# Linear attention plus feed-forward: a tail load on another queue, weights loaded twice, one transpose by DMA and a regrouped fold

## The chip, the cores and the metric

The kernel runs on one core of a Trainium2 chip. A core has a matrix engine (TensorE, PE in the profile; its weight loads are PEld), VectorE (DVE), ScalarE (ACT), GpSimd (POOL) and SyncE (SP), which run their own instruction streams and meet through semaphores, and 16 DMA engines, which move data on orders that SP and ACT issue. Each engine takes its instructions strictly in order. The metric is the device time of one execution in microseconds (us), as a median over runs.

## The reference

A normalised input goes into two branches whose outputs are added to the input. S = 2048 rows, D = 448 columns, 16 heads of 28, FF = 1792, all bf16:

```python
xn = layernorm(x)                                   # per row
q, k, v = split(xn @ wqkv)                          # 16 heads of 28 columns each
pq, pk = q @ w_phi[h], k @ w_phi[h]                 # the feature map, per head
phi_q = concat(softmax(pq), softmax(-pq)); phi_k = the same of pk
kv, z = phi_k^T v, sum of phi_k over the rows
o = (phi_q @ kv) / (phi_q . z + 1e-6)
out = x + o @ wo + silu(xn @ w1) @ w2
```

## The kernel before

The rows are worked on in 8 pairs of 128-row tiles (256 rows each). TensorE runs through these stages:

1. Normalisation of a pair (`ln_pair`): statistics and scaling on VectorE and GpSimd into `xn_sb` (two buffers), then a transpose into `xnT`, whose layout is two row groups of 64 partitions by seven blocks (448 = 7 x 64). Pairs 0 to 3 are transposed by TensorE (seven instructions, line 508) into PSUM bank 6 and evicted by VectorE (line 668). Pairs 4 to 7 are transposed by a DMA on SP's queue (line 561).
2. First feed-forward product (`ffn1_chunk`): xn @ w1, whose 14 column tiles go to silu on ScalarE. Column tiles 0 to 7 are done pair by pair (128-wide matmuls), 8 to 13 for two pairs at once (256-wide). Pairs 0 to 3 come in the first 36 us, pairs 4 to 7 later.
3. The fold (`fold`): the feature map is multiplied into the query and key weights. `wT` holds the transposed weights (eight DMA transposes from HBM, line 597; indices 4 to 7 for the keys and 0 to 3 for the queries), `BDphi` the block-diagonal feature map. Each of the two has four output blocks, done in groups of two with PSUM banks 4 and 7 (eight matmuls a group), evicted by ScalarE.
4. The K and V stage (`k_macro`, `q_group`, `k_acc`), which begins at 35.65 us in the trace and is called the value stage below: per pair the products for K, exponentials, V with its eviction on VectorE (line 800), the sums over the features, and the accumulation of kv. It takes until some 78 us.
5. The query stage with the second feed-forward product and the output, to the end.

Since TensorE contracts over 128 partitions in two halves of 64, a weight with 448 rows is stored twice, halves exchanged: a main load brings rows 0 to 383 into blocks 0 to 2 (`load_main`), a copy exchanges the 64-partition halves into blocks 3 to 5 (`swap`, two copies, one per half, each on ScalarE or VectorE), and the last 64 rows are loaded twice into block 6 (`load_tail`). This holds for w1 (`w1_sb`), the value weights (columns VO of `W_sb`) and wo; for the folded weights the swap follows the fold.

All loads of the first stages are issued by SP in the order in which they are written, but for the tail of w1's columns 0 to 512, which ACT issues behind its table load. The tail of the other columns of w1 is one pair of loads of 160 KB, issued directly behind the main load of columns 512 to 1024.

The order of every engine's instructions comes from a planner (`schedule`) that simulates the program with assumed durations: at each step it takes, among the operations that could start about first, the one with the lowest priority number and then the lowest number in the program, and fills gaps with others. A load's landing is planned from an assumed rate. TensorE also has 26 filler multiplications of a zero tile (`zz`, lines 545 to 551): 12 of 512 columns at the start and 14 of 256 columns that the planner puts into gaps. In the trace nine of the 14 stand behind pair 0's transposes, three and two on either side of pair 1's.

Of the kernel before, what the change touches and what calls it, by code (L numbers as in the profile page):

```python
# [8 lines left out]
ACTF = mybir.ActivationFunctionType  # L9
# [135 lines left out]
class _Prog:  # L145
# [72 lines left out]
    def schedule(self):  # L218
# [30 lines left out]
        for e, t0, per in (("sp", -100.0, 550.0), ("act", 1500.0, 600.0)):  # L249
            for q in loads[e]:  # L250
                t0 += ops[q[0]].dur if ops[q[0]].name == "wT_dt" else per
                q[2] = t0
        now, stalled = 0.0, False
# [111 lines left out]
def bass_parallel_sum__linear_kernel_hedgehog__dense_activation_silu__prompt_kernel(  # L365
# [20 lines left out]
    with es:  # L386
# [14 lines left out]
        WC = VO + D  # L401
# [70 lines left out]
        def d_dve(n, mode=1):  # L472
            return n * 1.042 / mode + 150.0
# [72 lines left out]
        for c0, c1 in ((0, 32), (32, 512)):  # L546
            P.op("dve", 450 + (c1 - c0) * 0.3, lambda e, c0=c0, c1=c1: e.memset(zz[:, c0:c1], 0.0), writes=[zz[:, c0:c1]], name="zz")
        for n, rows, cols, dur in ((12, 128, 512, 430.0), (0, 128, 512, 215.0), (14, 128, 256, 109.0)):
            for i in range(n):
                mm(banks[5][0:rows, 0:cols], zz[:, 0:rows], zz[:, 0:cols], True, True, "warm")  # L550
                P.ops[-1].dur = dur
# [8 lines left out]
        def transpose_dma(dst, src, name):  # L560
            P.dma(lambda e: e.dma_start_transpose(out=dst, in_=src), 128 * 896 * 2, reads=[src], writes=[dst], name=name, dur=1230.0)
# [4 lines left out]
        def load_main(dst, src, c0, c1, d0, name):  # L566
            load(dst[:, 0:3, d0:d0 + c1 - c0], src[0:384, c0:c1].rearrange("(k p) f -> p k f", p=128), 384 * (c1 - c0) * 2, name)

        def load_tail(dst, src, c0, c1, d0, name, eng="sp"):
            for h in range(2):  # L570
                o = load(dst[64 * h:64 * h + 64, d0:d0 + c1 - c0], src[384:448, c0:c1], 64 * (c1 - c0) * 2, name, eng, half=True)
                if eng == "act":
                    o.odeps.add(table_op.id)

# [13 lines left out]
        load_main(w1_sb, B_w1, 512, 1024, 512, "w1_1")  # L588
        load_tail(w1_sb[:, 6], B_w1, 512, FF, 512, "w1_1t")
        load_main(w1_sb, B_w1, 1024, 1408, 1024, "w1_2a")  # L590
        load_main(w1_sb, B_w1, 1408, FF, 1408, "w1_2b")
        load_x(2, 3)
# [12 lines left out]
        load_x(6, 8)  # L605
        load_main(W_sb, A_wqkv, 2 * D, 3 * D, VO, "wv")
        load_tail(W_sb[:, 6], A_wqkv, 2 * D, 3 * D, VO, "wvt")

# [8 lines left out]

        BK_F = [4, 7]
        first_ve, first_xn, first_ev, second_tr, second_ev, last_mm = [], [], [], [], [], []
# [38 lines left out]
        def ln_tr(p, bk):  # L658
            sl = p % NXN
            dstx = xnT[:, :, p, :]  # L660
            if p >= 4:
                transpose_dma(dstx, xn_sb[:, sl, :], "xnT_dt")
                return
            tp = bank16[bk][:, 0:896].rearrange("p (j c) -> p j c", j=KB)
            transpose_many([(tp[:, j, :], xn_sb[:, sl, 128 * j:128 * j + 128]) for j in range(KB)], "xnT_tr")
            if p == 1:
                second_tr.append(P.ops[-1])
            o = P.op("dve", d_dve(896, 2), lambda e: e.tensor_copy(dstx, tp), reads=[tp], writes=[dstx], name="xnT_ev")  # L668
            if p < 2:
                (first_ev, second_ev)[p].append(o)  # L670
# [56 lines left out]
        def fold():  # L727
# [9 lines left out]
            for a0 in range(0):  # L737
# [3 lines left out]
                for i in range(2):  # L741
                    act(wT[0:KP, a0 + 2 * i:a0 + 2 * i + 2], tps[i], ACTF.Identity, "wT_ev")
            swap(W_sb, VO, WC, ("dve", "dve"))
            for qk in (1, 0):
                for k0 in range(0, 4, 2):
                    parts = []
                    for i in range(2):
                        parts += [(banks[BK_F[i]][:, g * KP:(g + 1) * KP], wT[0:KP, qk * 4 + g, (k0 + i) * 128:(k0 + i + 1) * 128],
                                   BDphi[:, g, :], True, True) for g in range(G)]
                    mm_many(parts, "fold_mm")  # L750
                    for i in range(2):
                        dst, src = W_sb[:, k0 + i if k0 + i < 3 else 6, KO:VO], banks[BK_F[i]][:, 0:D]
                        if qk == 0:
                            dst = W_sb[:, k0 + i if k0 + i < 3 else 6, 0:QW].rearrange("p (g r f) -> p g r f", g=G, r=2)[:, :, :, 0:56]
                            src = src.rearrange("p (r g f) -> p g r f", r=2, g=G)
                        act(dst, src, ACTF.Identity, "fold_ev")
                swap(W_sb, KO if qk else 0, VO if qk else QW, ("dve", "dve"))

        ln_pair(0)
        swap(w1_sb, 0, 256, ("act", "act"))  # L760
        swap(w1_sb, 256, 512, ("act", "act"))
        ffn1_chunk(0, 1, 0, 4)
# [3 lines left out]
        ffn1_chunk(0, 1, 4, 8)  # L766
        last_mm[-1].odeps |= {q.id for q in second_tr}
        n0 = len(P.ops)
# [14 lines left out]
        ln_pair(5)  # L783
        ln_pair(6)
        ln_pair(7)

        def k_unit(p, j, b0, name):
# [334 lines left out]
```

## Time and profile before

| | us |
|---|---|
| median of 3 runs (157.63 to 158.75) | 158.08 |
| the profiled execution | 157.24 |
| its span | 155.5 |
| TensorE busy in the span | 150.7 (97%) |
| VectorE, ScalarE, GpSimd busy | 102.6, 74.2, 63.7 |
| chain that ended last: share of TensorE | 89% |
| start of the value stage (first matmul of `xnT` against folded weights) | 35.65 |

The span is the time from the first to the last instruction in the trace; 1.7 us of the execution lie around it. All times in the trace count from the start of the span. "idle before" in brackets is the time that an engine stood still ahead of an instruction, and behind it what ended that, as far as the trace shows. The chain is followed back from the last instruction: at each step to what released it, or to the instruction before on its engine.

### The profile page before, as it was taken

To read this page: it belongs to the slowest core of one execution; us is meant where nothing else is said; L and a number is where in the kernel's file an instruction comes from. 1 tells how busy PE (TensorE), PEld (TensorE's weight loads), DVE (VectorE), ACT (ScalarE), POOL (GpSimd) and SP (SyncE) were. 2 spreads that over 40 slices of the span, in tenths; PEclk is the share of its full clock that TensorE was granted. 3 is DMA by queue.
4 is the path that set the end of the run, shared out by engine and by line. 5 is a ranking of instruction groups with operands and counts; after the bars stand their busy time and mean duration, and the time that the engine had idled before them with its cause. 6 is when DMAs were issued, how large, how long until landed. Compare 5 with 4: busy or idle time off the path is not lost.

```text
span 155.5 us, 6049 instructions
## 1 busy us (share of the span) xinstructions
PE 150.7 (97%) x2751; PEld 98.3 (63%) x2751; DVE 102.6 (66%) x198; ACT 74.2 (48%) x82; POOL 63.7 (41%) x73
## 2 busy tenths in 40 slices
PE   6889999999999999999999999999999999999994
PEld 2378899795444546446878898655555555556553
DVE  5897977995978875889098769667985930022042
ACT  3778757878789688785955566800000000000000
POOL 5320306379388775479601453366146060000000
PEclk9999999999999999999999999999999999999999
DMA  5999678303724223300000083300840143041011
GB/s 152 268 277 115 110 180 249 62 17 69 99 53 139 49 93 95 93 0 6 4 4 4 0 63 63 59 4 0 124 118 4 28 115 98 0 118 63 0 59 59
DMA packets 23353, 12.11 MB, mean 78 GB/s; under 512 B 16160, under 2 KB 23200, under 8 KB 23328
## 3 DMA queue, kind: packets, MB, share of 16 engines
q1 hardware_dynamic: 23168, 11.60, 34.9%
q8 instruction: 21, 0.34, 0.9%
q10 hardware_dynamic: 160, 0.13, 0.3%
q14 instruction: 4, 0.03, 0.1%
HBM read 6.22 MB, written 1.84 MB: 52 GB/s over the span
## 4 chain that ended last, share of the span: by engine, by line
PE 89%; DVE 7%; POOL 2%; issue 1%; POOLq 0%
PE psum L490 84%; PE psum L483 4%; PE psum L508 1%; DVE st L621 1%; POOL rstd L637 1%; DVE KVZ L862 1%; DVE kvs L854 1%; DVE kvs L855 1%; DVE mask L532 1%; DVE xn_sb L650 1%; DVE mv L629 0%; DVE xnT L668 0%; DVE ve L635 0%; DVE KVZ L537 0%; POOL ident L519 0%
## 5 line engine op out<-in xcount | busy, mean ns | idle before, releaser
L490 PE MATMUL psum<-xnT,w_sb 64*128 64x256 bf16 (+1 forms) x1008 | 45.6, 246 | 0.5 <-DVE xn_sb L650 0.5
L490 PEld LDWEIGHTS psum<-xnT,w_sb 64*128 64x128 bf16 x1008 | 39.2, 94 | 5.0 <-ACT w_sb L515 0.6
L515 ACT ACTIVATE ar<-psum 128x896 bf16<-128x896 f32 (+2 forms) x38 | 32.0, 880 | 10.9 <-PE psum L490 10.8
L916 POOL TENSOR_TENSOR scr<-scr 128x384 bf16<-128x384 f32 (+3 forms) x32 | 20.1, 660 | 31.8 <-DVE scr L911 26.0
L808 POOL TENSOR_TENSOR ar<-ar,Rk 128x1792 bf16<-128x1792 bf16 (+1 forms) x9 | 25.8, 2877 | 10.1 <-DVE Rk L807 9.1
L960 DVE TENSOR_TENSOR out_sb<-psum,x_sb 128x448 bf16<-128x448 f32 (+2 forms) x17 | 9.5, 593 | 23.6 <-PE psum L490 20.5
L490 PE MATMUL psum<-ar,xnT 64*128 64x448 bf16 x224 | 22.7, 349 | 0.0
L490 PE MATMUL psum<-w_sb,hT_lo 64*128 64x448 bf16 x224 | 22.3, 349 | 0.0
L515 ACT ACTIVATE eq<-psum 128x1024 bf16<-128x1024 f32 x16 | 15.5, 1025 | 6.1 <-PE psum L490 6.0
L805 DVE TENSOR_REDUCE Sk<-ar 128x64 f32<-128x1792 bf16 (+1 forms) x9 | 16.2, 1804 | 2.5 <-ACT ar L515 2.5
L490 PEld LDWEIGHTS psum<-ar,xnT 64*128 64x128 bf16 x224 | 10.7, 94 | 10.4 <-DVE ar L800 0.4
L911 DVE TENSOR_TENSOR scr<-psum,Gq 128x896 f32<-128x896 f32 x16 | 16.9, 1087 | 0.4
L515 ACT ACTIVATE hT_lo<-psum 128x1024 bf16<-128x1024 f32 x14 | 14.3, 1022 | 5.9 <-PE psum L490 5.9
L490 PE MATMUL psum<-w_sb,ar 64*128 64x448 bf16 x168 | 16.6, 349 | 0.0
L490 PEld LDWEIGHTS psum<-w_sb,hT_lo 64*128 64x128 bf16 x224 | 10.5, 94 | 9.4
L637 POOL TENSOR_TENSOR rstd<-ve,neghalf 128x2 f32<-128x2 f32 (+1 forms) x9 | 6.2, 690 | 21.3 <-DVE ve L635 18.9
L490 PE MATMUL psum<-xnT,ar 64*128 64x512 bf16 x112 | 13.4, 376 | 0.0
L490 PEld LDWEIGHTS psum<-w_sb,ar 64*128 64x128 bf16 x168 | 8.4, 94 | 7.4
L490 PE MATMUL psum<-wo_sb,scr 64*128 64x448 bf16 (+2 forms) x119 | 11.9, 338 | 0.0
L800 DVE CAST ar<-psum 128x896 bf16<-128x896 f32 x8 | 8.6, 1069 | 4.0 <-PE psum L490 4.0
L621 DVE BATCH_NORM_STATS2 st<-x_sb 128x6 f32<-128x448 bf16 x16 | 9.7, 613 | 0.5 <-DMA x_sb<-in_A_x_dram 0.4
L650 POOL TENSOR_SCALAR xn_sb<-x_sb,mv,rstd 128x192 bf16<-128x192 bf16 (+1 forms) x8 | 9.5, 1190 | 0.4
(50 smaller groups left out, 119.4 us busy)
## 6 DMA issues: line engine op xcount, KB each, us to landing
out_dram<-out_sb SPq DMA_DIRECT2D x7, 224.0 KB, 2.2
x_sb<-in_A_x_dram SPq DMA_DIRECT2D x4, 224.0 KB, 5.4
x_sb<-in_A_x_dram SPq DMA_DIRECT2D x2, 448.0 KB, 4.8
w_sb<-in_B_w_dram SPq DMA_DIRECT2D x2, 448.0 KB, 3.6
w_sb<-in_B_w_dram SPq DMA_DIRECT2D x2, 336.0 KB, 3.4
w_sb<-in_B_w_dram SPq DMA_DIRECT2D x2, 288.0 KB, 6.6
w_sb<-in_B_w_dram SPq DMA_DIRECT2D x2, 192.0 KB, 3.4
w_sb<-in_B_w_dram SPq DMA_DIRECT2D x1, 384.0 KB, 6.5
```

Of the source, the lines that this page charges most:

```text
L483: lambda e: e.matmul(dst, lhsT, rhs, start=start, stop=stop, skip_group_check=True),
L490: r = e.matmul(dst, lhsT, rhs, start=start, stop=stop, skip_group_check=True)
L515: return P.op("act", d_act(_cols(src)), lambda e: e.activation(dst, src, func, scale=scale), reads=[src], writes=[dst], table=table, name= ...
L621: o = P.op("dve", 630, lambda e: e.bn_stats(st6[:, t, :], x_sb[:, t, :]), reads=[x_sb[:, t, :]], writes=[st6[:, t, :]], name="bnst")
L637: P.op("pool", 580, lambda e: e.tensor_tensor(r2, v2, nh, ALU.pow), reads=[v2, nh], writes=[r2], name="rstd")
L650: o = P.op("pool" if pool else "dve", 150 + _cols(xs) * 1.6 if pool else 120 + _cols(xs) * 0.6, lambda e, xn=xn, xs=xs: e.tensor_scalar(xn ...
L800: P.op("dve", d_dve(896), lambda e: e.tensor_copy(dstv, vb), reads=[vb], writes=[dstv], name="v_ev")
L805: P.op("dve", d_dve(896 * n), lambda e, S3=S3, E3=E3: e.tensor_reduce(S3, E3, AXL.X, ALU.add), reads=[E3], writes=[S3], name="Sk")
L808: P.op("pool", d_pool(896 * n, 1.77), lambda e, E3=E3, R3=R3, n=n: e.tensor_tensor(E3, E3, R3[:, :, None].broadcast_to([128, 32 * n, DH]), ...
L911: P.op("dve", d_dve(896), lambda e, dsto=dsto, Us=Us, Gs=Gs: e.tensor_tensor(dsto, Us, Gs[:, :, :, :, None].broadcast_to([128, 2, 2, 8, DH ...
L916: P.op("pool", d_pool(_cols(a0), 2.26), lambda e, dst=dst, a0=a0, a1=a1: e.tensor_tensor(dst, a0, a1, ALU.add), reads=[a0, a1], writes=[ds ...
L960: P.op("dve", d_dve(c1 - c0), lambda e: e.tensor_tensor(dst, ob, xs, ALU.add), reads=[ob, xs], writes=[dst], name="out_ev")
```

## The change

- w1's tail rows for columns 512 to 1024 are loaded by ACT's queue (two loads of 64 KB), behind the two copies of columns 0 to 256. Those for columns 1024 to 1792 stay on SP (two loads of 96 KB) but are issued behind the main load of columns 1024 to 1408.
- The value weights are loaded a second time with the halves exchanged (`load_swapped`, two loads of 168 KB on SP), and the two swap copies on VectorE are dropped.
- Pair 3 is transposed by a DMA on SP's queue. On SP it stands behind the load of x for pairs 6 and 7 and ahead of the value weights.
- The fold works on four output blocks at a time, in PSUM banks 4 to 7; VectorE evicts every second block.
- Fillers of 256 columns: 9 in place of 14. Those left stand behind pair 0's transposes.
- The planner assumes other landing times for ACT's loads, pair 7's normalisation gets a lower priority, and one order rule of pair 1's transposes names the last matmul group but one.

In the new order TensorE does the 16 fold matmuls of the keys directly behind the 112 matmuls of pair 1, then 98 matmuls of pair 2, the 16 fold matmuls of the queries, 14 more of pair 2, and then the 256-wide matmuls of pairs 2 and 3, the first that read pair 3. On VectorE the copy that duplicates the queries' `wT` (line 736) and the swaps of the folded weights stand ahead of pair 4's normalisation, and the first V eviction stands ahead of pair 7's.

```diff
-            for q in loads[e]:
+            for i, q in enumerate(loads[e]):
                 t0 += ops[q[0]].dur if ops[q[0]].name == "wT_dt" else per
-                q[2] = t0
+                q[2] = t0 if e == "sp" or i < 2 else max(t0, 4300.0 + 600.0 * (i - 1))
...
-        for n, rows, cols, dur in ((12, 128, 512, 430.0), (0, 128, 512, 215.0), (14, 128, 256, 109.0)):
+        for n, rows, cols, dur in ((12, 128, 512, 430.0), (0, 128, 512, 215.0), (9, 128, 256, 109.0)):
...
-        def load_tail(dst, src, c0, c1, d0, name, eng="sp"):
+        def load_tail(dst, src, c0, c1, d0, name, eng="sp", after=table_op):
             for h in range(2):
                 o = load(dst[64 * h:64 * h + 64, d0:d0 + c1 - c0], src[384:448, c0:c1], 64 * (c1 - c0) * 2, name, eng, half=True)
                 if eng == "act":
-                    o.odeps.add(table_op.id)
+                    o.odeps.add(after.id)
+
+        def load_swapped(dst, src, c0, c1, d0, name):
+            for h in range(2):
+                rows = src[0:384, c0:c1].rearrange("(k b p) f -> b p k f", b=2, p=64)[1 - h]
+                load(dst[64 * h:64 * h + 64, 3:6, d0:d0 + c1 - c0], rows, 192 * (c1 - c0) * 2, name, half=True)
...
         load_main(w1_sb, B_w1, 512, 1024, 512, "w1_1")
-        load_tail(w1_sb[:, 6], B_w1, 512, FF, 512, "w1_1t")
         load_main(w1_sb, B_w1, 1024, 1408, 1024, "w1_2a")
+        load_tail(w1_sb[:, 6], B_w1, 1024, FF, 1024, "w1_2t")
         load_main(w1_sb, B_w1, 1408, FF, 1408, "w1_2b")
...
         load_main(W_sb, A_wqkv, 2 * D, 3 * D, VO, "wv")
+        load_swapped(W_sb, A_wqkv, 2 * D, 3 * D, VO, "wvs")
         load_tail(W_sb[:, 6], A_wqkv, 2 * D, 3 * D, VO, "wvt")
...
-        BK_F = [4, 7]
+        BK_F = [4, 5, 6, 7]
...
-            if p >= 4:
+            if p >= 3:
                 transpose_dma(dstx, xn_sb[:, sl, :], "xnT_dt")
+                if p < 4:
+                    P.ops[-1].prio = -1
                 return
...
-            swap(W_sb, VO, WC, ("dve", "dve"))
             for qk in (1, 0):
-                for k0 in range(0, 4, 2):
+                for k0 in range(0, 4, 4):
                     parts = []
-                    for i in range(2):
+                    for i in range(4):
...
-                        act(dst, src, ACTF.Identity, "fold_ev")
+                        if i % 2:
+                            P.op("dve", d_dve(D), lambda e, dst=dst, src=src: e.tensor_copy(dst, src), reads=[src], writes=[dst], name="fold_ev")
+                        else:
+                            act(dst, src, ACTF.Identity, "fold_ev")
...
         swap(w1_sb, 0, 256, ("act", "act"))
+        load_tail(w1_sb[:, 6], B_w1, 512, 1024, 512, "w1_1t", "act", P.ops[-1])
         swap(w1_sb, 256, 512, ("act", "act"))
...
-        last_mm[-1].odeps |= {q.id for q in second_tr}
+        last_mm[-2].odeps |= {q.id for q in second_tr}
...
+        P.cur_prio = 1
         ln_pair(7)
+        P.cur_prio = 0
```

More of the change, by code (lines that the diff above doesn't have):

```diff
@@ L750, in fold @@
                     mm_many(parts, "fold_mm")
-                    for i in range(2):
+                    for i in range(4):
                         dst, src = W_sb[:, k0 + i if k0 + i < 3 else 6, KO:VO], banks[BK_F[i]][:, 0:D]
```

## The prediction

> **What bounds the kernel now.** I read the slices of the page first: TensorE (PE) is at 9 tenths from the fourth slice to the last but one and its granted clock is at 9 throughout, so the time is the length of TensorE's own program plus its few gaps. Then I read the chain of waits, because it says which instructions of that program are on the path. Columns: start us, us, what.
>
> ```profile
> 10.23 0.39 DVE xn_sb L650
> 10.62 0.12 issue
> 10.74 1.35 PE psum L490 x42
> 12.09 0.43 PE psum L483 x3
> 12.53 0.39 PE psum L508 x7
> 12.92 0.50 PE psum L490 x14
> 13.42 0.32 PE psum L483 x2
> 13.74 4.69 PE psum L490 x84
> 18.43 0.50 PE psum L508 x7
> 18.93 3.23 PE psum L490 x112
> 22.16 0.50 PE psum L508 x7
> 22.66 51.56 PE psum L490 x1130
> ```
>
> From 10.74 to 74.22 the chain is TensorE alone. So every matmul taken out of this stretch shortens the run, and every wait put into it lengthens it one for one. L483 are filler multiplications of zeros (0.43 and 0.32), L508 the transposes of one pair's input (0.50 each).
>
> Third, the rows of the transfers and of what waits for them, since three parts of the change move transfers. From the DMA view in narrow windows (tile, queue, count, size, us from issue to landing) and the timeline:
>
> ```profile
> w_sb<-in_B_w_dram SPq DMA_DIRECT2D x1, 384.0 KB, 6.5
> w_sb<-in_B_w_dram SPq DMA_DIRECT2D x2, 160.0 KB, 6.5
> ...
> x_sb<-in_A_x_dram SPq DMA_DIRECT2D x1, 448.0 KB, 5.1
> ar<-in_A_wqkv_dram SPq DMA_DIRECT2D x1, 336.0 KB, 5.8
> ...
> xnT<-xn_sb SPq DMA_TRANSPOSE x1, 2.9
> ```
>
> ```profile
> 21.22 0.58 SPq L555 DMA_DIRECT2D x_sb<-in_A_x_dram  x1
> 21.84 2.49 SPq L555 DMA_DIRECT2D ar<-in_A_wqkv_dram  x3
> 25.20 0.23 DVE L736 COPY eq<-eq 112x256 bf16<-112x256 bf16 x1 [0.85 <-DMA eq<-in_A_wqkv_dram]
> ```
>
> The reader is to see that SP's queue is backlogged here: a load issued at 21.84 lands at 27.6, and VectorE (DVE) waited for the last query weights wT until 25.2.
>
> **First part: w1's tail rows.** TensorE ran 56 matmuls from 8.55 for 1.74 us, was free at 10.29 and started the next at 10.74. The chain names the normalisation, but that step isn't an operand. The operands are w1's columns 512 to 1024: the main rows (384 KB, issued 2.7, landed 9.2), their ScalarE (ACT) copy (two from 9.26 in 1.58 us, so the first ends at 10.05), and the tail rows of 160 KB (the second issued about 4.15, landed about 10.65). The last of these ends the wait. The change sends 64 KB pieces of that tail by ACT's queue, after the second copy at 3.82, so by 5.5. The two 64 KB pieces on that queue at the start took 3.5 and 4.0 us, their issues 0.6 each; the second would land by 6.1 + 4.0 = 10.1. ACT loses at most 0.3 us: its next copy started at 6.43 and would start at 6.75, ending at 8.5, and TensorE needs it at 9.4. But the pieces now flow beside the main rows: 128 KB at the slice's 277 GB/s is 0.47 us, so the main rows land at 9.2 to 9.7 and TensorE starts between 10.3 and 10.65. Gain 0.1 to 0.4.
>
> Here a rule weighs against the change. The Trainium skill, "DMA: Bandwidth & Descriptors", section "Issuing engines are not separate DMA queues", says that DMAs from several engines run on the same 16 DMA engines and interleave, so that a second issuer saves only issue time. By it the lower end, 0.1, would hold.
>
> **Second part: filler.** Five of fourteen fillers go (the nine at 7.47 stay, beside VectorE's eviction). The three at 12.09 are 0.43 on the chain. The two at 13.42 cover the eviction of pair 1 (ends 13.58), so they give 0.1. Behind them, ACT's copy of columns 1024 to 1408 (the first of two from 11.65 in 2.20, ending 12.75, or 13.2 if the main rows came late) now holds the start of the 84 matmuls to 12.9 or 13.3 in place of 13.7. Front gain in all: 0.4 to 0.8, taken as 0.6. The clock could fall in a larger gap; the two gaps there are now (0.53 and 0.45) show 1.00, so I give that nothing. The tail of columns 1024 to 1792 goes behind one main load; up to there fewer bytes are queued, and the later main load has the same bytes ahead of it as before.
>
> **Third part: pair 3's transposes.** Seven transposes (0.50) leave TensorE and an eviction (0.62) leaves VectorE. In their place stands a DMA transpose on SP's queue, and TensorE's first 256-wide matmul of pairs 2 and 3 waits for it. When is it needed? The 112 matmuls now end at 22.16; with the front gain, 21.56. Then come, in the new order, 16 fold matmuls (8 take 0.50, from 24.66 to 25.16, so 1.0), 98 matmuls (98/112 of 3.23 = 2.83), to 25.4; then 16 fold matmuls that need the wT copy of the row above (25.20 + 0.23 and a semaphore: 25.5). The transfers ahead of wT are the same, so this holds whatever the front gained above 0.5. Fold to 26.5, 14 matmuls (0.4): needed at 26.9. If it is there, 84 matmuls (4.69) and 112 (3.23) follow, and the value stage begins at 34.8; before it began at 35.65. So the whole change is worth at most 0.83 us.
>
> When does it land? Pair 3's rows are normalised by 20.04 + 1.08 = 21.1, so SP doesn't wait, and issues it after the 448 KB of x at 21.8. An empty queue gave 2.9 us (pair 4, issued 27.94): landing at 24.7. The load that was issued at this very place took 5.8: 27.6. The x load ahead lands at 21.2 + 5.1 = 26.3; a whole 2.9 behind it is 29.2. I take 27.6, since the backlog is the same, and keep 24.7 and 29.2 for the range. Against 26.9 that is a wait of 0.8 (with 0.1 for the semaphore), which gives back the 0.83.
>
> A page speaks here too. The Trainium skill, "Advanced Engine Details and Errata", section "X-Bar Transpose (TRN2)", says that transpose DMAs are as fast as regular ones. The case's rows don't agree: 112 KB of wT took 4.2 to 5.2 us to land among loads of 448 KB that took 4.4 and 5.1. By the page the 224 KB would be through half a microsecond or so behind x, at 26.9, and the run would be about 0.7 faster.
>
> **Fourth part: value weights.** The two V swaps on VectorE go (of four copies in 2.60: 1.30 us), two strided loads of 168 KB come, behind the transpose. SP's issues then run to about 27.5 (0.6 each, 1.25 for the transpose); even with 5.8 us to land, all is there by 33, and the first V product is near 37. Free, unless the queue backs up by 4 us. Pair 4's transpose isn't ready before that.
>
> **Fifth part: the fold.** The same 32 matmuls, in two groups of 16, and half of the evictions (ACT 0.97 for two) on VectorE. As ACT has pauses of 0.23 to 0.67 between all its steps there, what it loses is nothing on the path. VectorE gains four evictions of about 0.6 (bounds 0.49, ACT's, and 0.64, its PSUM copy of 464 columns): +2.4, -1.30, -0.62: +0.5. The order matters more: the copy that waits for wT, and behind it two swaps, now stand ahead of pair 4's normalisation, which moves from 25.9 to about 30.4; GpSimd's share and the transposes of pairs 4 to 7 behind it on SP move too. Pair 4 is first read some 18 us after the value stage begins, so ten microseconds are spare. What has less room is the first V eviction (38.55 to 39.63): it stands behind pair 6's normalisation, and I reach 38.3 for its start, as VectorE's idle 1.81 us ahead of 38.02 covers the lateness. Its banks are next written near 41.2 (the second pair's products start at 39.81, half of 2.81 on), so 1.6 us are spare; beyond that each microsecond would be TensorE's.
>
> **Sum.** The profiled execution took 157.24 (span 155.5 and 1.7 around it), 0.84 below the median of 158.08. Front 0.4 to 0.8, transposes 0.5, cut to 0.83 by wT, less 0.8 for pair 3: 0.0. So 157.2 against the profiled run, 158.0 against the median.
>
> **Rivals.** (a) Pair 3 lands in time, 26.8 or sooner: the 0.83 stays, 157.25. For it: 2.9 us on an empty queue. Against: every transfer issued between 21.2 and 24.3 took 5.1 to 5.8. (b) Slower: the transpose's last pieces hang as those of wT did where a load followed directly. The last wT, ahead of x, took 5.2, the one before it 4.3: 0.9 more. With wv right behind, 27.6 + 0.9 = 28.5 means a wait of 1.7, net 0.87 slower: 158.95; at 29.2 it is 1.6 slower, 159.65. The point from which this decides is a landing at 27.65. (c) VectorE's new order makes the first value evictions late: pair 6 normalised 2.5 us later than I reach uses up the 1.6 and gives 0.9 on TensorE, 158.9. (d) The first part does nothing, since ACT's pieces only push the main rows: front gain 0.4 at the least, and wT hides most of the difference: 158.1, within the forecast.
>
> **How the numbers follow.** About no change, with (d): 0.47 (own range 157.6 to 158.5). (a): 0.25. (b): 0.22. (c): 0.06. The range takes in (a) and most of (b): 157.1 to 159.5. One per cent, 1.6 us, is about what a measurement here can tell from no change. Faster by more than that needs wT to come earlier as well, 0.06; slower needs (b) at its end or (b) and (c) together, 0.13; within 0.81.
>
> **What would show it.** In the new profile: the gap before the 42 matmuls gone or under 0.3; the 84 matmuls starting near 13.1; the second fold group starting near 25.5; then a wait of TensorE for the transpose of xnT, and its landing after 27. The value stage starts at 35.6 by the forecast, 34.8 by (a), 36.5 by (b). I am wrong if TensorE waits inside the value stage, if the clock falls below 1.00, or if wT lands elsewhere than at 25.

## The result and the profile after

The changed kernel takes 160.31 us (median of 20 runs, 158.11 to 162.63), the kernel before in the same comparison 157.59 (20 runs, 156.42 to 159.06): slower by a ratio of 1.0124, 95% interval 1.0094 to 1.0153. That is outside the range of the prediction. Two things must be known to read the numbers below: the profiled execution of the changed kernel took 158.11, the shortest of its 20, so a second profile of the same kernel, of 159.84 us, is shown beside it; and the ratios leave out executions more than 1.5% above the shortest of their kernel, so for a kernel that spreads as this one does they can differ from the quotient of the medians.

The chain of waits of the changed kernel (start us, us, what), the answer to the chain shown of the kernel before:

```profile
35.57 4.20 DMA xnT<-xn_sb
...
39.87 0.70 DVE xn_sb L656 x2
40.56 1.94 DVE Sk L818
...
42.52 0.55 DVE Rk L820
43.08 0.96 DVE ar L813
...
44.08 9.32 PE psum L490 x207
```

Before, everything from 10.74 to 74.22 was TensorE. Now the chain leaves TensorE in the value stage: a transpose of pair 5 holds a buffer, behind it VectorE normalises pair 7, sums features (Sk, Rk) and only then evicts a V product (`ar`, line 813), and TensorE starts behind that at 44.08. TensorE's timeline, with what ended the idle time in brackets:

```profile
8.54 3.17 PE L490 MATMUL psum<-xnT,w_sb 64*128 64x128 bf16 x98
34.23 2.81 PE L490 MATMUL psum<-ar,xnT 64*128 64x448 bf16 x28
39.06 2.82 PE L490 MATMUL psum<-ar,xnT 64*128 64x448 bf16 x28 [0.51 <-DVE ar L813]
44.08 2.82 PE L490 MATMUL psum<-ar,xnT 64*128 64x448 bf16 x28 [0.69 <-DVE ar L813]
```

The front did better here than I forecast: the 56 and 42 matmuls run as 98 without a gap, and the value stage begins at 34.23, not at 35.6. Then come two waits for V evictions. The kernel before, TensorE's timeline, VectorE's first V eviction, and the first matmul of the query stage in the kernel before and in the changed one:

```profile
35.65 2.81 PE L490 MATMUL psum<-ar,xnT 64*128 64x448 bf16 x28
39.81 2.81 PE L490 MATMUL psum<-ar,xnT 64*128 64x448 bf16 x28
38.55 1.08 DVE L800 CAST ar<-psum 128x896 bf16<-128x896 f32 x1
81.69 0.63 PE L490 MATMUL psum<-KVZ,eq 56*128 56x60 bf16 x32 [0.20 <-DVE KVZ L862]
82.27 0.63 PE L490 MATMUL psum<-KVZ,eq 56*128 56x60 bf16 x32 [0.20 <-DVE KVZ L875]
```

One pair takes 4.16 us in the kernel before (35.65 to 39.81); here 34.23 to 39.06 is 0.67 more and 39.06 to 44.08 is 0.86 more. From the start of the value stage to the first matmul of the query stage it is 48.04 us, before 46.04. VectorE's timeline says why the evictions (line 813) come when they do:

```profile
36.27 0.70 DVE L656 TENSOR_SCALAR xn_sb<-x_sb,mv,rstd 128x384 bf16<-128x384 bf16 x2 [0.69 <-POOL rstd L643]
37.92 1.08 DVE L813 CAST ar<-psum 128x896 bf16<-128x896 f32 x1
39.87 0.70 DVE L656 TENSOR_SCALAR xn_sb<-x_sb,mv,rstd 128x384 bf16<-128x384 bf16 x2 [0.87 <-DMA xnT<-xn_sb]
40.48 2.01 DVE L818 TENSOR_REDUCE Sk<-ar 128x64 f32<-128x1792 bf16 x1
42.99 1.03 DVE L813 CAST ar<-psum 128x896 bf16<-128x896 f32 x1
```

The first eviction ends at 39.00 and TensorE starts at 39.06. Before, it ended at 39.63 and the next pair's matmuls started at 39.81: there was never any room. The written order takes the next pair's V product ahead of its K product, so the first matmul of the pair writes just the banks that this eviction frees. ScalarE's exponentials of the pair show the order: in the kernel before they start at 42.67, when all 28 matmuls are done (42.62), not behind the first 14 (41.30).

The second profile of the same kernel, TensorE's timeline:

```profile
11.40 1.35 PE L490 MATMUL psum<-xnT,w_sb 64*128 64x128 bf16 x42 [1.11 <-ACT hT_lo L515]
27.05 0.57 PE L490 MATMUL psum<-BDphi,eq 112*128 112x112 bf16 x8 [0.36 <-issue]
35.79 2.81 PE L490 MATMUL psum<-ar,xnT 64*128 64x448 bf16 x28
40.62 2.82 PE L490 MATMUL psum<-ar,xnT 64*128 64x448 bf16 x28 [0.51 <-DVE ar L813]
45.83 2.82 PE L490 MATMUL psum<-ar,xnT 64*128 64x448 bf16 x28 [0.87 <-DVE ar L813]
55.31 0.82 PE L490 MATMUL psum<-xnT,ar 64*128 64x512 bf16 x5 [0.15 <-issue]
```

Here the 42 matmuls wait 1.11 us, more than the 0.45 of before, whose row is

```profile
10.74 1.35 PE L490 MATMUL psum<-xnT,w_sb 64*128 64x128 bf16 x42 [0.45 <-DVE xn_sb L650]
```

and the value stage starts at 35.79, where the forecast had it. The waits for V evictions are about as in the first profile, so they don't come from its short time; and twice TensorE stands with nothing to wait for ("issue"). The wait at the 42 matmuls is that for w1's new tail pieces: in all 20 profiles taken, those of the experiments among them, TensorE starts these matmuls 0.14 us behind the landing of the second tail piece (10.61 and 10.74 in the kernel before, 11.26 and 11.40 here), whichever releaser the timeline names. From the DMA view in a narrow window, first profile, then the second (size, us from issue to landing):

```profile
w_sb<-in_B_w_dram ACTq DMA_DIRECT2D x2, 64.0 KB, 5.7
xnT<-xn_sb SPq DMA_TRANSPOSE x1, 4.9
```

```profile
w_sb<-in_B_w_dram ACTq DMA_DIRECT2D x2, 64.0 KB, 6.7
xnT<-xn_sb SPq DMA_TRANSPOSE x1, 5.9
```

The pieces are issued at 4.0 and some 4.5 on ACT's queue in both. The second lands at 10.2 in one and 11.3 in the other. Pair 3's transpose, issued at 21.01 and 21.61, lands at 25.9 and 27.5, and TensorE waits for it in neither.

### The profile page after: what moved, and what is told of

Same layout as the page of the kernel before. It is cut to its first block, busy times and chain, and to the rows that moved or that the text cites. A ratio compares the mean times of both kernels' runs of the same rounds, so it can differ in the third digit from the quotient of the medians.

```text
span 156.0 us, 6031 instructions
## 1 busy us (share of the span) xinstructions
PE 149.9 (96%) x2739; PEld 98.0 (63%) x2739; DVE 103.6 (66%) x199; ACT 72.5 (46%) x78; POOL 63.4 (41%) x73
## 4 chain that ended last, share of the span: by engine, by line
PE 68%; DVE 5%; DMA 3%; issue 0%; DVEq 0%
PE psum L490 64%; PE psum L483 3%; DMA xnT<-xn_sb 3%; DVE Sk L818 1%; DVE kvs L867 1%; DVE KVZ L875 1%; DVE kvs L868 1%; DVE ar L813 1%; DVE xn_sb L656 0%; DVE Rk L820 0%; DVE out_sb L973 0%; DVEq L1075 0%
## 5 line engine op out<-in xcount | busy, mean ns | idle before, releaser
L515 ACT ACTIVATE ar<-psum 128x896 bf16<-128x896 f32 (+2 forms) x34 | 30.0, 920 | 13.0 <-PE psum L490 13.0
L490 PE MATMUL psum<-xnT,ar 64*128 64x512 bf16 x112 | 14.0, 377 | 0.0
```

The lines of the kernel that those rows point to most:

```text
L490: r = e.matmul(dst, lhsT, rhs, start=start, stop=stop, skip_group_check=True)
L515: return P.op("act", d_act(_cols(src)), lambda e: e.activation(dst, src, func, scale=scale), reads=[src], writes=[dst], table=table, name= ...
```

## The experiments

Three suspects: w1's tail pieces come late on ACT's queue; VectorE comes late to the V evictions; pair 3's transpose holds something. Diffs are against the changed kernel where nothing else is said.

**The changed kernel again**, no edit.

> The changed kernel once more, to have its time beside the others of this chip and, with luck, a profile of an execution of the usual length: its median was 160.3 us, and the one profile so far is of an execution of 158.1. Theory T1 (pair 3's DMA transpose lands late in most executions): in a profile of a long execution TensorE stands still 1.5 to 2.5 us near 26 us, and the value stage begins after 36. Theory T2 (VectorE's queue stands behind the normalisation of pair 7, which waits for pair 5's transpose to free its buffer): the value stage begins near 34.2 as before, and the first two V evictions are later, with waits of TensorE of 2 to 4 us in all between 38 and 48. Time: 158 to 161.

Measured 159.90 us, ratio 1.0139 (1.0095 to 1.0183); its profile is the second one above. T1's wait for pair 3 isn't there. T2's waits are, but smaller than it said (0.51 and 0.87), and the value stage doesn't begin early.

**Pair 3 back on TensorE.**

```diff
-            if p >= 3:
+            if p >= 4:
```

> Pair 3 is transposed by TensorE again; all else of the change stays. The seven transposes cost TensorE 0.5 us, and pair 4's normalisation has a free buffer. T1: the long executions vanish, 157 us at the median. T2: pairs 4 to 7 still come late on VectorE, so a part stays; 158.5 to 160.

160.59, ratio 1.0144 (1.009 to 1.0197): outside the ranges of both theories. Undoing this one alone gives nothing. The waits for V evictions stay, 0.33 and 1.01; the wait ahead of the 42 matmuls was 1.76 in this profile.

**Three buffers for the normalised rows**, so that pair 7 doesn't wait for pair 5's transpose.

```diff
-        NXN = 2
+        NXN = 3
```

> Three buffers for the normalised rows in place of two, in the same order of instructions on every engine. Pair 7's normalisation then needs pair 4's transpose, not pair 5's. T2: it starts with the reciprocal root of GpSimd near 39.4 us, the waits of TensorE at the V products shrink below 0.9 us in all, and the median falls by 1.5 to 2.5 us, to 158 to 158.8. T1: nothing but 0.4 us changes, 160.

159.67, ratio 1.0085 (1.005 to 1.0119). The second V wait shrank from 0.87 to 0.26, but not to nothing: pair 7 then waits for GpSimd (0.44). By the ratio it gains 0.5%, by the medians 0.1%, and the intervals overlap, so a gain isn't shown. In this profile the 42 matmuls waited 1.98 and the two idle stretches were 1.19 and 0.52.

**Pair 7 normalised ahead of the first V eviction.**

```diff
-        P.cur_prio = 1
         ln_pair(7)
-        P.cur_prio = 0
```

> Pair 7's normalisation at the old priority: on VectorE it stands ahead of the first V eviction instead of behind it. T2: worse, since the first V eviction now also waits for pair 5's transpose: 0.8 to 2 us slower than the changed kernel. T1: no difference beyond 0.5 us from the changed kernel.

162.49, ratio 1.0271 (1.0217 to 1.0326): one wait of 2.89 us for the first V eviction, which now stands behind pair 7's wait of 1.68 for its buffer. TensorE's timeline:

```profile
43.72 4.17 PE L490 MATMUL psum<-ar,xnT 64*128 64x448 bf16 x28 [2.89 <-DVE ar L811]
```

Behind this wait the matmuls are slower too (28 of them take 4.17 where 2.82 is usual; the clock is at the end of this document). What VectorE does ahead of that eviction is on the path; the change's lower priority for pair 7 is a remedy.

**The tail back on SP's queue.**

```diff
+        load_tail(w1_sb[:, 6], B_w1, 512, FF, 512, "w1_1t")
         load_main(w1_sb, B_w1, 1024, 1408, 1024, "w1_2a")
-        load_tail(w1_sb[:, 6], B_w1, 1024, FF, 1024, "w1_2t")
...
-        load_tail(w1_sb[:, 6], B_w1, 512, 1024, 512, "w1_1t", "act", P.ops[-1])
```

In this and in every other run that moves the tail, the planner's landing times for ACT's loads move with it.

> The changed kernel with w1's tail rows 512 to 1792 back on SP's queue, in two pieces of 160 KB directly behind the main load of columns 512 to 1024, as before the change. Theory A (the pieces on ScalarE's queue land 6.6 to 7.5 us after issue in most executions and hold up the 42 matmuls by 1.0 to 2.0 us, where SP's pieces cost 0.45): the wait ahead of the 42 matmuls is 0.6 or less, the waits for the V evictions of 1.2 to 1.9 us in the value stage stay, and the time is 158.4 to 159.2, ratio to the kernel before 1.005 to 1.010. Rival B (only VectorE's later order costs, and what is saved at the front is lost there anyway): within 0.3 us of the changed kernel, ratio 1.011 to 1.015.

159.76, ratio 1.0113 (1.0069 to 1.0158): 0.25% less than the 1.0139 of the changed kernel's second run, inside the intervals of both. The profile has a wait of 1.13 at the 42 matmuls, so SP's order doesn't exclude one.

**The old fold.**

```diff
-        BK_F = [4, 5, 6, 7]
+        BK_F = [4, 7]
...
-                for k0 in range(0, 4, 4):
+                for k0 in range(0, 4, 2):
...
```

All evictions of the fold go back to ScalarE with it.

> The changed kernel with the fold as before the change: four groups of eight matmuls on two banks, all evictions on ScalarE. Theory B (the fold's evictions and swaps on VectorE ahead of pair 4's normalisation make the first two V evictions late, 1.2 to 1.9 us of waits of TensorE in the value stage): pair 4 is normalised near 26 and not near 30, the two waits shrink to 0.4 or less together, and the time is 158.2 to 159.0, ratio 1.004 to 1.009; the wait ahead of the 42 matmuls stays at 1.0 to 2.0 in a profile of usual length. Rival A (only the late w1 pieces cost): ratio 1.011 to 1.015. A third (TensorE stands for an instruction fetch of 0.4 to 1.2 us inside the second group of 16 fold matmuls): that gap is gone or shifts to the rows behind it.

160.49, ratio 1.0199 (1.0154 to 1.0244). A miss as a remedy, but its profile is clear (TensorE's timeline, then VectorE's):

```profile
27.52 0.94 PE L490 MATMUL psum<-xnT,w_sb 64*128 64x256 bf16 x14 [1.28 <-DMA xnT<-xn_sb]
36.46 2.81 PE L490 MATMUL psum<-ar,xnT 64*128 64x448 bf16 x28
40.62 2.81 PE L490 MATMUL psum<-ar,xnT 64*128 64x448 bf16 x28
55.12 0.82 PE L490 MATMUL psum<-xnT,ar 64*128 64x512 bf16 x6 [1.24 <-issue]
```

```profile
39.31 1.09 DVE L810 CAST ar<-psum 128x896 bf16<-128x896 f32 x1 [2.17 <-PE psum L490]
```

The V waits are gone (36.46 to 40.62 is the undisturbed 4.16), so in this company the new fold's work on VectorE does bring them. That TensorE comes later here doesn't explain it: VectorE stood ready 2.17 us ahead of the first V eviction, more than the 1.28 that TensorE lost. In their place TensorE waits 1.28 for pair 3: in the old grouping its first reader comes earlier. The new fold is what hides the new transpose.

**The tail on ACT's queue alone, on the kernel before.**

```diff
-        load_tail(w1_sb[:, 6], B_w1, 512, FF, 512, "w1_1t")
         load_main(w1_sb, B_w1, 1024, 1408, 1024, "w1_2a")
+        load_tail(w1_sb[:, 6], B_w1, 1024, FF, 1024, "w1_2t")
...
+        load_tail(w1_sb[:, 6], B_w1, 512, 1024, 512, "w1_1t", "act", P.ops[-1])
```

> The kernel before with one part of the change alone: w1's tail rows 512 to 1024 in two pieces of 64 KB on ScalarE's queue behind the second copy, the rest of the tail on SP behind the main load of columns 1024 to 1408; all fillers and the rest as before. Theory A: the wait ahead of the 42 matmuls is 1.0 us or more in most executions, 158.1 to 159.0, ratio 1.003 to 1.009, and single times spread over more than 2 us. Rival (the pieces on ScalarE's queue are harmless, as the profiled execution of 158.11 us shows them, and the loss is all in the later stages): ratio 0.996 to 1.001.

159.10, ratio 1.0096 (1.0065 to 1.0127); the spread of more than 2 us didn't show (158.52 to 159.53). TensorE's timeline, and the DMA view of the transfers that the 42 matmuls need (both pieces with their median, the second alone, the main rows):

```profile
12.51 1.35 PE L490 MATMUL psum<-xnT,w_sb 64*128 64x128 bf16 x42 [1.85 <-DVE xn_sb L650]
```

```profile
w_sb<-in_B_w_dram ACTq DMA_DIRECT2D x2, 64.0 KB, 7.2
w_sb<-in_B_w_dram ACTq DMA_DIRECT2D x1, 64.0 KB, 7.9
w_sb<-in_B_w_dram SPq DMA_DIRECT2D x1, 384.0 KB, 8.1
```

The page names VectorE's normalisation, which isn't an operand. The second piece, issued at 4.49, lands at 12.37, and TensorE starts at 12.51. The main rows took 8.1 us where the kernel before shows 6.5, and landed at 10.8.

**Tail and fold both undone.**

```diff
-        load_tail(w1_sb[:, 6], B_w1, 512, 1024, 512, "w1_1t", "act", P.ops[-1])
...
-        BK_F = [4, 5, 6, 7]
+        BK_F = [4, 7]
```

> The changed kernel with both undone: w1's tail on SP's queue as before, and the fold in four groups as before. Five fillers less, pair 3's transpose by DMA and the value weights loaded twice stay. Theories A and B together: no wait for w1 above 0.6, waits for V evictions under 0.4, value stage at 34.8 to 35.3, 156.8 to 157.5, ratio 0.994 to 1.000. If the transpose of pair 3 or the second load of the value weights costs by itself: 158.0 or more, ratio over 1.003.

160.54, ratio 1.0166 (1.012 to 1.0212): another miss. TensorE's timeline:

```profile
29.11 1.23 PE L490 MATMUL psum<-xnT,w_sb 64*128 64x256 bf16 x14 [2.14 <-DMA xnT<-xn_sb]
```

It waited 2.14 for pair 3's transpose, and the matmuls behind that wait ran slower for a while.

**The other four parts, each alone on the kernel before.** The value weights loaded twice:

```diff
+        load_swapped(W_sb, A_wqkv, 2 * D, 3 * D, VO, "wvs")
...
-            swap(W_sb, VO, WC, ("dve", "dve"))
```

> The kernel before with one part of the change alone: the value weights' rows loaded a second time in swapped places (two loads of 168 KB), in place of the two copies on VectorE. Theory C (336 KB more on the transfer engines delay TensorE's instruction fetch, so that it stands 0.2 to 1.2 us with nothing to wait for among the matmuls near 54): such an idle stretch shows, and the time is 157.8 to 158.7, ratio 1.002 to 1.007. Rival (free, as the prediction had it): no such stretch, 157.1 to 157.8, ratio 0.997 to 1.001.

157.97, ratio 1.0003 (0.997 to 1.0036): free, and no idle stretch of TensorE in its profile. The fold in two groups:

```diff
-        BK_F = [4, 7]
+        BK_F = [4, 5, 6, 7]
...
+                        if i % 2:
+                            P.op("dve", d_dve(D), lambda e, dst=dst, src=src: e.tensor_copy(dst, src), ...)
```

> The kernel before with one part of the change alone: the fold in two groups of 16 on four banks, half of its evictions on VectorE. Theory B (VectorE gets to the first V evictions too late): TensorE waits 0.8 to 1.9 us for the V evictions of the first two pairs, 158.4 to 159.5, ratio 1.005 to 1.012. Rival (the waits need the other parts too: pair 3's transpose on SP's queue, the early front): no such waits, ratio 0.998 to 1.002.

158.08, ratio 1.0012 (0.9983 to 1.004). No V wait, although VectorE gets to the eviction even later: 3.84 us behind the start of the value stage (35.43), 3.69 in both profiles of the changed kernel, 2.90 in the kernel before. VectorE's timeline, then TensorE's:

```profile
39.27 1.08 DVE L803 CAST ar<-psum 128x896 bf16<-128x896 f32 x1
```

```profile
39.75 2.82 PE L490 MATMUL psum<-ar,xnT 64*128 64x448 bf16 x28
```

TensorE starts the second pair at 39.75, before the eviction ends at 40.35. The planner took this pair's K product first, which uses other banks (ScalarE's exponentials start at 41.62, behind the first 14 matmuls); presumably it saw VectorE this late in its simulation. So this run doesn't price the new fold as it stands in the changed kernel, where V comes first. Pair 3 by DMA:

```diff
-            if p >= 4:
+            if p >= 3:
```

> The kernel before with one part of the change alone: pair 3's input transposed by DMA, with the old fold in four groups. The first matmuls on pairs 2 and 3 together come before the third fold group here, some 2.3 us earlier than in the changed kernel. Theory D (the new grouping of the fold is what hides this transpose): TensorE waits 1.0 to 2.2 us for it, less 0.5 for the seven transposes saved: 158.2 to 159.3, ratio 1.003 to 1.011. Rival (the transpose lands early enough by itself and the seven transposes are saved): 156.8 to 157.5, ratio 0.995 to 0.999.

159.11, ratio 1.0044 (1.0005 to 1.0082). TensorE's timeline, then VectorE's:

```profile
27.76 0.94 PE L490 MATMUL psum<-xnT,w_sb 64*128 64x256 bf16 x14 [1.32 <-DMA xnT<-xn_sb]
41.85 2.82 PE L490 MATMUL psum<-ar,xnT 64*128 64x448 bf16 x28 [0.83 <-DVE ar L802]
55.25 1.25 PE L490 MATMUL psum<-xnT,ar 64*128 64x512 bf16 x10 [0.56 <-issue]
```

```profile
29.81 1.27 DVE L581 COPY ar<-ar 64x1344 bf16<-64x1344 bf16 x2 [2.72 <-DMA ar<-in_A_wqkv_dram]
```

All three kinds of wait are here: for the transpose itself, for a V eviction, and for nothing visible. The V wait has a cause of its own: VectorE's swaps of the value weights waited 2.72 us, since their load now stands behind the transpose on SP's queue (issued at 23.08 in place of 21.84, landed at 29.79 in place of 27.63). The changed kernel has no such swaps, so this wait is no price of the transpose there. Five fillers less:

```diff
-((12, 128, 512, 430.0), (0, 128, 512, 215.0), (14, 128, 256, 109.0))
+((12, 128, 512, 430.0), (0, 128, 512, 215.0), (9, 128, 256, 109.0))
```

> The kernel before with one part of the change alone: nine of the fourteen filler multiplications, the five behind the first 98 matmuls left out. Prediction's price: 0.43 and 0.1 less on TensorE's path, 157.0 to 157.4, ratio 0.996 to 0.999. Rival (they only cover waits, for VectorE's eviction and ScalarE's copy, that stand there without them too): 157.4 to 157.8, ratio 0.999 to 1.002.

157.44, ratio 0.9971 (0.9939 to 1.0002), 0.46 us at the middle. Its profile has a V wait of 0.26 and an idle stretch of 0.77, so the earlier front runs into both. The five ratios add up to 0.96 + 0.44 + 0.12 + 0.03 - 0.29 = 1.26%, about the whole loss of 1.24%. That they meet is partly luck: each interval is about 0.3% to either side, and the fold (K first) and pair 3 (a wait for the value weights) cost other things alone than in company. The order rule of pair 1's transposes wasn't tried by itself.

**K product first.** Does VectorE or TensorE's own order make the V waits? In the changed kernel:

```diff
             k_unit(p, 1, 0, "pk")
+            pk = P.ops[-1]
...
             k_unit(p, 2, 2, "v")
+            if p in (1, 2):
+                P.ops[-1].odeps.add(pk.id)
```

> The changed kernel with one order more on TensorE: of pairs 1 and 2 the K product comes before the V product. VectorE's, ScalarE's and GpSimd's orders are as in the changed kernel. Theory E (the two waits come from the place of the V product, which needs its banks back 1.4 us sooner than the K product would let it): the waits of 0.5 and 0.7 to 0.9 us are gone or under 0.2 together, 158.4 to 159.2, ratio 1.004 to 1.009. Rival (VectorE's or the other chain's lateness bounds the stage, and a wait for the exponentials or for pair 7 takes their place): another wait of about the same size, ratio 1.011 to 1.015.

160.03, ratio 1.0136 (1.0096 to 1.0176). Right about the waits, wrong about the time. TensorE's timeline, and busy time with the granted clock (PEclk) by windows of 2 us:

```profile
12.36 2.31 PE L490 MATMUL psum<-xnT,w_sb 64*128 64x128 bf16 x42 [2.07 <-DMA w_sb<-in_B_w_dram]
56.86 0.82 PE L490 MATMUL psum<-xnT,ar 64*128 64x512 bf16 x5 [1.47 <-issue]
```

```profile
12.00:14.00 2.00, 1.64 (x35) 1.67 (x37) 0.63 (x2) 2.00 (x3) 0.00 (x0) 0.63 1.62 50
14.00:16.00 2.00, 2.00 (x32) 1.61 (x29) 0.44 (x1) 0.80 (x1) 0.00 (x0) 0.51 0.95 167
16.00:18.00 2.00, 1.99 (x40) 1.63 (x36) 1.90 (x5) 1.04 (x2) 0.00 (x0) 1.00 0.75 63
```

No wait for a V eviction is left; the first pair takes 4.32 (37.58 to 41.90), 0.16 more than 4.16, as K's banks come free with ScalarE's second exponential of the pair (it ends at 41.85). But w1's pieces cost 2.07 us, and the clock fell to half behind that gap (the 42 matmuls took 2.31, not 1.35). At 56.86 an idle stretch of 1.47 stands where the second profile of the changed kernel has 0.15. Next, the tail on SP's queue as well:

```diff
+        load_tail(w1_sb[:, 6], B_w1, 512, FF, 512, "w1_1t")
...
-        load_tail(w1_sb[:, 6], B_w1, 512, 1024, 512, "w1_1t", "act", P.ops[-1])
```

> The kernel with the K products first, and w1's tail rows back on SP's queue in two pieces of 160 KB. Theory A (the tail on ScalarE's queue costs by itself, 0.25 to 0.96% by the two runs so far): 157.2 to 158.4, ratio 0.997 to 1.004, and the wait ahead of the 42 matmuls at 0.2 to 1.1 us. Rival (the tail's place costs nothing in the changed kernel, since later transfers bound the stage): within 0.2% of the kernel with the K products first alone.

158.63, ratio 1.0064 (1.0033 to 1.0095), 0.7% less. And three buffers on top:

```diff
-        NXN = 2
+        NXN = 3
```

> The kernel with the K products first and the tail on SP's queue, and three buffers for the normalised rows in place of two. Theory F (the buffer holds VectorE on the path even now): 0.3 to 0.5% under the kernel without the third buffer. Rival (the buffer mattered only through the V evictions' waits, which are gone): the same within 0.2%.

158.15, ratio 1.0014 (0.9988 to 1.0041): about 0.5% less, with intervals that overlap. In place of that, on the kernel with two buffers, pair 3 back on TensorE:

```diff
-            if p >= 3:
+            if p >= 4:
```

> The kernel with the K products first and the tail on SP's queue, and pair 3's input transposed by TensorE as before the change; what is left of the change is the fold in two groups, five fillers less, the value weights loaded twice and pair 7's later place. Theory G (pair 3's transpose by DMA carries most of what remains, 0.4% alone): ratio 0.996 to 1.002, 157.2 to 158.2. Rival (the fold's two groups, or the instruction fetch that TensorE stands for at some 54 us, carry it): ratio 1.004 to 1.009.

157.62, ratio 0.9995 (0.9967 to 1.0023): the loss is gone, with the new fold, the value weights loaded twice, five fillers less and pair 7's later place still in. TensorE's timeline with pair 3 by DMA, and then with pair 3 on TensorE:

```profile
34.52 2.83 PE L490 MATMUL psum<-ar,xnT 64*128 64x448 bf16 x28
54.20 0.80 PE L490 MATMUL psum<-xnT,ar 64*128 64x512 bf16 x5 [1.61 <-issue]
```

```profile
35.34 2.81 PE L490 MATMUL psum<-ar,xnT 64*128 64x448 bf16 x28
39.67 2.82 PE L490 MATMUL psum<-ar,xnT 64*128 64x448 bf16 x28
```

With the transpose by DMA the value stage starts 0.82 us earlier (0.29 of it was there at the 42 matmuls already, so about the 0.50 of the seven transposes is left); then 1.61 us pass at 54 that the other doesn't have. The spans, 156.5 and 155.7, differ by just that balance.

**The two harmless parts together, on the kernel before**, and the same with the K products first:

```diff
-((12, 128, 512, 430.0), (0, 128, 512, 215.0), (14, 128, 256, 109.0))
+((12, 128, 512, 430.0), (0, 128, 512, 215.0), (9, 128, 256, 109.0))
...
+        load_swapped(W_sb, A_wqkv, 2 * D, 3 * D, VO, "wvs")
...
-            swap(W_sb, VO, WC, ("dve", "dve"))
```

> The kernel before with the two parts of the change that cost nothing alone: five fillers less, and the value weights loaded twice in place of two copies on VectorE. If the parts add: 157.2 to 157.7, ratio 0.995 to 0.999. If the earlier front only runs into a later wait: 157.7 to 158.1, ratio 1.000 to 1.002. The wait ahead of the 42 matmuls, whose loads are those of the kernel before: 0.2 to 0.9 us.

157.38, ratio 0.9963 (0.9935 to 0.999): the one kernel here whose interval lies below the kernel before.

```diff
             k_unit(p, 2, 2, "v")
+            if p in (1, 2):
+                P.ops[-1].odeps.add(pk.id)
```

> The kernel before with five fillers less and the value weights loaded twice, and the K product first in pairs 1 and 2. If the order only matters where VectorE is late (theory E): the same as without it within 0.3%, ratio 0.994 to 0.999. Rival (the V evictions are so tight in the kernel before that K first saves there too): ratio 0.990 to 0.994.

158.10, ratio 1.001 (0.9985 to 1.0036), above both ranges. Where VectorE is on time, K first saves nothing and costs a little: the first pair takes 4.32 (35.40 to 39.72), and an idle stretch of 0.20 came with it.

**What the profiles say together.** The wait ahead of the 42 matmuls in all 20 profiles, the two of the changed kernel and the one of the kernel before among them (us):

| w1's tail | profiles | waits | mean | main rows, us to landing | second tail piece lands behind the main rows by |
|---|---|---|---|---|---|
| SP's queue | 12 | 0.45 1.13 1.00 0.94 0.44 0.39 0.21 0.56 0.27 0.61 0.55 0.24 | 0.57 | 6.3 to 7.3, mean 6.7 | 1.2 to 1.6, mean 1.33 |
| ACT's queue | 8 | 0 1.11 1.76 1.98 1.01 0.57 1.85 2.07 | 1.29 | 5.3 to 8.1, mean 6.7 | 1.6 to 2.4, mean 2.14 |

So it isn't the main rows that make the difference, but the tail behind them. In all eight profiles with ACT's queue the second piece, issued at about 4.5, lands behind two transfers that SP issued sooner: the 288 KB of columns 1024 to 1408 (issued at 3.44) and the first 96 KB of the other tail (4.1). In the twelve others the tail stands ahead of those 288 KB and lands before them. From the main rows on, up to and with the piece that ends the wait, 896 KB are issued in place of 704; 192 KB at the 277 GB/s of the prediction is 0.71 us, and the table shows 0.81. That is an estimate from these rows; no run put the tail behind those 288 KB on SP's queue to test it.

The idle stretches with nothing to wait for, summed over a profile up to the query stage: with pair 3 by DMA eleven profiles, 0 to 1.71 us, 1.0 on average; with pair 3 on TensorE nine, 0 to 0.77, 0.24 on average. By the trace's count, wherever such a stretch lies TensorE has done 472, 980 to 982, or 1492 to 1493 matmuls since the start (fillers and transposes counted): some 510 from one place to the next, whichever kernel it is.

## Why the prediction was wrong

**First part: the failed step of the largest size.** "The second would land by 6.1 + 4.0 = 10.1." The 4.0 us was the time of pieces sent at the very start. The second is issued earlier than I put it (by 4.6) and takes 5.7 to 7.9 us, behind loads that SP issued before it, so it lands at 10.2 to 12.4; and its landing is what ends the wait in every profile. That the pieces push the main rows, the only price that I gave them, doesn't show (landed at 9.4 on average with either queue). In place of a gain of 0.1 to 0.4 the runs show a loss: 0.96% alone (1.5 us), 0.7% (1.1 us) where the K products come first, of which the means of the table (1.29 less 0.57) give 0.7 us; when the gap passes 2 us the clock takes more. The sentence on a second issuer that shares the same engines pointed the right way, and even its lower end was too good.

**Fifth part: the failed step of the mechanism.** "Its banks are next written near 41.2 ... so 1.6 us are spare." I took the K product to come first in the second pair. V comes first and the banks are needed at once: 0.2 us of room in the kernel before, and 0.6 where I saw 1.6 (an eviction from 38.3 ends at 39.4, the matmuls follow 4.16 behind 35.79, at 39.95). VectorE's lateness I under-sized too, by the second profile, whose value stage starts where I had it: pair 4 is normalised at 31.46 (forecast 30.4), the first V eviction starts at 39.48 (38.3). With the spare that I claimed this would still have been covered. Putting K first removed the waits, which shows their cause, though by itself it didn't shorten the run (1.0136); rival (c) had the mechanism, and I gave it 0.06 on the false spare. I also missed the second wait: pair 7 stands ahead of the second eviction, and waits for pair 5's transpose to free one of two buffers (0.87 to 0.26 with a third).

**Third part: landing about right, wait absent, price elsewhere.** Forecast 27.6; landed 25.9 and 27.5 in the two profiles of the changed kernel, up to 28.7 with three buffers. The wait of 0.8 wasn't there, since TensorE came later itself; with K first, tail on SP and three buffers it was 0.81. wT's copy (24.18 and 25.22) held nothing, against my floor of 25.5; so 0.83 wasn't the most that could be had: 34.23 is 1.42 ahead of 35.65. Alone the part costs 0.44%, through the three waits shown above. In company it costs 0.7%: between the profiles that differ in it alone that is the idle stretch of 1.61 less 0.82 at the front, and idle stretches I hadn't thought of.

**Right:** fillers (0.53 forecast, 0.46 measured, interval 0 to 1.0), value weights (nothing; nothing). The sign that I named of being wrong, a wait inside the value stage, is there. The value stage at 35.6 (35.79 in the profile of 159.84) is luck: I had a front gain of 0.6 and a wait of 0.8 for pair 3; that profile has a loss at the 42 matmuls, no wait for pair 3, and an idle stretch of 0.36. The loss of 2.3 us of span in that profile lies behind this mark: 1.72 in the two V waits (35.79 to 40.62 and on to 45.83, less 4.16 each), 0.15 at 55.31, the rest in small pieces.

**Open.** The idle stretches fall 12 matmuls later in kernels that have 12 matmuls less on TensorE, that is, at the fixed counts given above, and end 2.2 to 3.4 us after a 16 KB packet on the queue that the DMA view calls "instruction". So TensorE probably waits for its next instructions there; that is read from the traces, not tested. Why they come later with pair 3 by DMA isn't known; moving the place by padding the program wasn't tried. The effects of the tail and of K first, taken alone in the changed kernel (0.25% and 0.03% below 1.0139), are smaller than together (0.75%); intervals of 0.4% each don't decide whether one stretch of waiting covers the other.

## What to carry to other kernels

Before a wait is called covered, look up which product writes the freed banks next in the written order, not which could; the margin is the difference of two lines in the trace, and here it was 0.2 us. A load's time is taken from one that was issued at the same moment among the same traffic, not from the same size on an empty queue. Before a load moves to another queue, look up what is issued ahead of it there. And try each part of a change alone and in company: two of five cost nothing alone, and together they took 0.4% off the kernel that all five made slower.

## What the runs showed of the hardware

- A gap of 2.07 us ahead of the 42 matmuls halved the granted clock for some 3.4 us (0.63 and 0.51 in two windows of 2 us); gaps of 2.14 (tail and fold undone; 0.50 from 30 to 33 us) and 2.89 (pair 7 first) did the same, one of 1.98 did not. Behind the gap of 2.89, which ended at 43.72, the clock still showed 1.00 from 44 to 45 us, then 0.51 from 45 to 46 and 0.50 from 46 to 48. The Trainium skill, "TensorE: Matmul & The Clock Gate", section "What's actually happening", has the clock fall after an idle window of about 3.4 us. The length of the slow stretch agrees; the idle time that was enough was shorter here.
- The same 384 KB of w1, issued 2.7 us into the program, took 5.3 to 8.1 us from one kernel and execution to the next.
- In the middle of a group of matmuls TensorE stood up to 1.61 us with nothing that the profile shows to wait for, at fixed counts of its matmuls some 510 apart, and in some kernels not at all.
- 64 KB issued at 4.5 us on ACT's queue landed behind 288 KB and 96 KB that SP had issued at 3.44 and 4.1, in eight profiles of eight.
